# The end of a spectral-mix kernel: a tile's maximum and both of its products in one PSUM bank

## Chip, cores and metric

The kernel runs on one core of a Trainium2 chip. The metric is device time in microseconds (us): the median of several executions for the comparison, and one profiled execution for the trace. TensorE is called PE here, VectorE DVE, ScalarE ACT, GpSimd POOL; SP issues most transfers.

## What is computed

An attention over a sliding window with a linear position bias gives x; a spectral mix of 64 modes gives y; the end joins them. Cut to what matters (B 8, H 8, S 576, D 64, so 512 channels):

```python
x = attention(q, k, v)                    # window 128, bias by head; [8, 576, 512]
X = rfft(x, axis=1)[:, :64]               # 64 modes
Yr = Xr @ w_r - Xi @ w_i                  # one 512x512 matrix for each mode
Yi = Xr @ w_i + Xi @ w_r
y = irfft(Y, n=S, axis=1)
u = x + y
out = u + maximum(u @ w_ch, 0)            # fp32, [8, 576, 512]
```

The two weight tensors are 134 MB of fp32, read once; the output is 9.4 MB.

## The kernel before, in words

The first part is the attention by units of a head pair and a batch. Beside and after it the weights come through a ring of 12288 fp32 words a partition, each load two modes of one of w_r or w_i; `_load_w` issues a load on SP's queue as soon as `_modes` has used the place that it overwrites. `_modes` multiplies the chosen spectrum (Xz) by one load, 24 products into `acc`, and every few modes DVE adds `acc` into ZT, the spectrum of y laid out by channel.

During the weight stage the kernel does by the way what it can for the end. The output is 36 tiles of 128 rows by 512 channels (`g.seq`): for each batch four whole tiles, and for each two batches one tile of their two last half tiles. For each tile `_xt` transposes x and `_xw` multiplies it by w_ch; ACT and DVE split the result in two bf16 parts, high and low, and keep them in `hl`. `_z_early` turns the ZT of one batch into Z (rows are modes, columns channels) and ZW, which is Z times w_ch. The rows of the last modes are not there yet; they come as "late rows" after the last weights, for four batches at a time (`_z_late`), through a bf16 copy `zl` (`_z_late_out`), and `_z_put` copies 32 rows of it into place in Z and ZW.

With FT, the inverse transform, a tile's y is FT times Z and its y @ w_ch is FT times ZW. Products for a tile come in pairs, one for each half of 64 rows. A tile goes one of two ways (`g.way`):

- "a" (19 tiles): PE adds hl and FT times ZW in bank `mm`, and x (by the identity) and FT times Z in bank `y`: four pairs. ACT takes the relu of `mm`, DVE adds `y`.
- "q" (17 tiles): here x was added into hl already, by one identity product in `_xw`. PE makes `mm` from hl and FT times ZW, and `y` from FT times Z: three pairs. ACT copies `y`, DVE takes the maximum of `mm` and x (which is x + relu), POOL adds the two.

`_known` makes what needs no Z (lines 842 to 856), `_taken` what needs Z and ZW (829 to 839). The first two tiles (KNOWN) are made without the late rows in PE's idle time before the last weights, and the late rows added after. `_finish` (859 to 912) runs over the tiles in a hand-written order: every engine's queue is in the order of the code. The late rows of batches 0 to 3 are put by POOL, those of batches 4 to 7 are made after tile 7 (LATE_AT) and put by ACT and DVE at fixed tiles (PUT_Z). A "q" tile's transfer is issued after that of the next "a" tile.

Of the kernel before, what the change touches and what calls it, by code (L numbers as in the profile page):

```python
# [16 lines left out]
P = 128  # L17
# [9 lines left out]
TAIL = 2  # L27
XW = (20, 63)
EARLY_Z = (53, 55, 57, 58, 59, 60, 61, 62)
KNOWN = 2  # L30
FT_ROWS = (2, 3, 4, 5, 6)
FT_ORDERS = (10, 14, 18, 22)
WCH_ROWS = (1, 4)
PUT_Z = {4: 9, 5: 11, 6: 13, 7: 15}
LATE_AT = 7
SUMS = (P, 3 * P, 4 * P)


class Ctx:
# [4 lines left out]
def kernel(  # L44
# [44 lines left out]
    for b in range(B):  # L89
# [3 lines left out]
        if b == B - 1:  # L93
            t = [t[4], t[1], t[0], t[3], t[2]]
        g.seq += t
    g.way = ["q" if i > 4 and t[1][0][1] in SUMS and i != len(g.seq) - 5 else "a"
             for i, t in enumerate(g.seq)]

    with tc.manual_schedule(engines={ET.SP, ET.PE, ET.Activation, ET.DVE, ET.Pool}):
        with ExitStack() as wctx:  # L100
# [5 lines left out]
            with ExitStack() as actx:  # L106
# [87 lines left out]
                tc.tile_pool(name="eps", bufs=1, space=bass.MemoryType.PSUM))  # L194
            g.fps = ctx.enter_context(
                tc.tile_pool(name="fps", bufs=1, space=bass.MemoryType.PSUM))
            g.mm, g.y = {}, {}
            _select(g, last, 0)
            rest_w = [(m, w) for m in range(0, NM, 2) for w in range(2)]
            with ExitStack() as xctx:  # L200
# [28 lines left out]
            for m0, w in rest_w:  # L229
                _modes(g, last, m0, w, last=True)  # L230
                done = m0 + w + 1
                if done in EARLY_Z:
                    _z_early(g, EARLY_Z.index(done))
                if done == NM - 1:
                    for i in range(KNOWN):
                        _known(g, i)
                        _taken(g, i, last=False)
            _known(g, KNOWN, (1,))
            mctx.close()
        _finish(g)  # L240

# [319 lines left out]
def _select(g, j, m0):  # L561


    nc = g.nc
    A, H = len(GROUPS[j]), JOINT[j]
    pool = g.zp if j else g.work
    X = pool.tile([P, H * A, 3, MB, g.B], BF16, tag=f"Xz{j}", bufs=2, name=f"Xz{j}")
    per = H // len(GROUPS) if j else H
    for o0 in range(0, H, per):
        if j:  # L570
            ps = g.fps.tile([P, g.DM], FP32, tag=("mm", "y")[o0], name="xz")
        else:
            ps = g.ps2.tile([P, g.DM], FP32, tag="xt", name="xz")
        w = 2 * A * MB * g.B
        for o in range(per):
            q = ps[:, o * w : o * w + w].rearrange("p (c m b) -> p c m b", m=MB, b=g.B)
            for h in range(H):
                nc.tensor.matmul(  # L578
                    q[:, :, h::H], lhsT=g.sel[j][:, o0 + o, h],
                    rhs=g.Xn[j].rearrange("p c i b m -> p (c i) m b")[:, :, m0 + h : m0 + MB : H],  # L580
                    start=True, stop=True)
        q = ps[:, 0 : per * w].rearrange("p (c i m b) -> p c i m b", i=2, m=MB, b=g.B)
        r = slice(A * o0, A * (o0 + per))
        nc.vector.tensor_copy(X[:, r, 1:3], q)  # L584
        nc.scalar.mul(X[:, r, 0], q[:, :, 1], -1.0)  # L585
    g.X[j, m0 // MB] = X
# [58 lines left out]
def _load_w(g):  # L645
# [6 lines left out]
    for u, z in g.place[g.used : g.loaded]:  # L652
# [2 lines left out]
    g.loaded += 1  # L655
    r0 = GROUPS[j][0] * P
    src = (g.w_r, g.w_i)[w][m0 : m0 + JOINT[j], r0 : r0 + len(GROUPS[j]) * P]
    g.nc.sync.dma_start(
        out=g.ring[:, lo:hi], in_=src.rearrange("m (p a) e -> p m (a e)", a=ROWS[j]))
    return True  # L660


# [20 lines left out]
def _modes(g, j, m0, w, last=False):  # L683
# [9 lines left out]
        g.acc[j] = (m0, g.mpsum.tile([P, 4, 2, MB, 8], FP32, tag="acc", name="acc"))  # L693
    c0, acc = g.acc[j]
    R, n = ROWS[j], JOINT[j]
    for et in range(4):
        for a in range(R):
            nc.tensor.matmul(  # L698
                acc[:, et, :, m0 - c0 : m0 - c0 + n, :],
                lhsT=wt[:, a, et * P : (et + 1) * P],  # L700
                rhs=X[:, a, 1 - w : 3 - w, m0 % MB : m0 % MB + n],
                start=(m0 == c0 and w == et == a == 0),
                stop=(m0 + n in ends and w == 1 and et == 3 and a == R - 1))
    g.used += 1
    while _load_w(g):
        pass
# [36 lines left out]
def _xw(g, n, xT, psum):  # L743
# [2 lines left out]
    nc = g.nc  # L746
    x = g.seq[n][0]
    xw = psum.tile([P, g.DM], FP32, tag="xw", bufs=2, name="xw")
    if g.way[n] == "q":
        nc.tensor.matmul(xw, lhsT=g.ident_b, rhs=x, start=True, stop=False)  # L750
    for dt in range(4):
        nc.tensor.matmul(  # L752
            xw, lhsT=xT[:, dt], rhs=g.wch[:, dt],
            start=(dt == 0 and g.way[n] != "q"), stop=(dt == 3))
    for h in range(2):
        own, other = (slice(64 * i, 64 * i + 64) for i in (h, 1 - h))
        nc.scalar.copy(g.hl[own, n, h], xw[own])  # L757
# [4 lines left out]
def _z_early(g, b):  # L762
# [10 lines left out]
                _z_product(g, ps, w, et, k, l)  # L773
    nc.vector.tensor_copy(g.Z[b], zp.rearrange("p a b -> p (a b)"))
    nc.scalar.copy(g.ZW[b], zwp)  # L775
    if b == 0:
        nc.vector.memset(g.Z[b][0:32], 0.0)
        nc.gpsimd.memset(g.ZW[b][0:32], 0.0)  # L778


def _z_product(g, ps, w, et, k, l):
# [25 lines left out]
def _z_late_out(g, pool):  # L807

    nc = g.nc
    t = [pool.tile([P, g.DM], BF16, tag=f"zl{w}", bufs=1, name=f"zl{w}") for w in range(2)]  # L810
    nc.vector.tensor_copy(t[0], g.late[0])
    nc.scalar.copy(t[1], g.late[1])
    g.late = t


def _z_put(g, b):

    nc = g.nc
    ks = slice(32 * (b % 4), 32 * (b % 4) + 32)
    for z, t, odd in ((g.ZW, g.late[1], False), (g.Z, g.late[0], b % 2)):  # L820
        if b < 4:
            nc.gpsimd.tensor_copy(z[b][ks], t[ks])
        elif odd:
            nc.vector.tensor_copy(z[b][ks], t[ks])
        else:
            nc.scalar.copy(z[b][ks], t[ks])


def _taken(g, i, late=None, last=True):

    nc = g.nc
    rows = slice(0, 32) if late else slice(0, P)
    for w, out in ((1, g.mm[i]), (0, g.y[i])):
        for h, (b, s) in enumerate(g.seq[i][1]):
            z = late[w] if late else (g.Z, g.ZW)[w][b]
            nc.tensor.matmul(  # L836
                out[64 * h : 64 * h + 64], lhsT=g.FT[rows, b % 4, s : s + 64], rhs=z[rows],
                start=(w == 0 and g.way[i] == "q" and not late), stop=last,
                tile_position=(0, 64 * h))


def _known(g, i, which=(1, 0)):

    nc = g.nc
    x = g.seq[i][0]
    if 1 in which:
        pool = g.lps if i % 3 else g.fps
        g.mm[i] = pool.tile([P, g.DM], FP32, tag="mm", bufs=2 if i % 3 else 1, name="mm")
        _pair(nc, g.mm[i], [g.ident2] * 2, [g.hl[:, i, h] for h in range(2)],
              start=True, stop=False)  # L850
    if 0 in which:
        pool = g.fps if i % 3 == 0 else g.lps if i % 3 == 1 else g.kps
        g.y[i] = pool.tile([P, g.DM], FP32, tag="y", name="y")
        if g.way[i] == "a":
            _pair(nc, g.y[i], [g.ident_b[:, 0:64], g.ident_b[:, 64:128]], [x] * 2,
                  start=True, stop=False)


def _finish(g):

    nc, tc = g.nc, g.tc
    N = len(g.seq)
    with ExitStack() as fctx:
        pool = fctx.enter_context(tc.tile_pool(name="fin", bufs=4))
        g.kps = fctx.enter_context(
            tc.tile_pool(name="kps", bufs=1, space=bass.MemoryType.PSUM, side="right"))
        _z_late(g, 0)
        _known(g, KNOWN, (0,))  # L870
        _z_late_out(g, pool)
        first, ready = g.late, []
        for b in range(4):
            _z_put(g, b)
        for i in range(N + 1):
            if i < N:
                if i < KNOWN:
                    _taken(g, i, first)
                else:
                    if i > KNOWN:  # L880
                        _known(g, i)
                    _taken(g, i)
            if i == LATE_AT:
                _z_late(g, 4)
            j = i - 1
            if j < 0:
                continue
            x, (lo, hi) = g.seq[j]
            whole = hi == (lo[0], lo[1] + 64)
            oj = pool.tile([P, g.DM], FP32, tag="o", bufs=11, name="o")  # L890
            if g.way[j] == "a":
                r = pool.tile([P, g.DM], FP32, tag="r", name="r")
                nc.scalar.activation(r, g.mm[j], AF.Relu)
                nc.vector.tensor_tensor(out=oj, in0=g.y[j], in1=r, op=ALU.add)
            else:
                ys = pool.tile([P, g.DM], FP32, tag="y", name="ys")
                nc.scalar.copy(ys, g.y[j])
                r = pool.tile([P, g.DM], FP32, tag="r", name="r")
                nc.vector.tensor_tensor(out=r, in0=g.mm[j], in1=x, op=ALU.max)
                nc.gpsimd.tensor_tensor(out=oj, in0=r, in1=ys, op=ALU.add)  # L900
            ready.append((oj, lo, hi, whole))
            if g.way[j] == "a":
                for oj, lo, hi, whole in ready[-1:] + ready[:-1]:
                    if whole:
                        nc.sync.dma_start(out=g.out[lo[0], lo[1] : lo[1] + P], in_=oj)
                        continue
                    for h, (b, s) in enumerate((lo, hi)):
                        nc.sync.dma_start(out=g.out[b, s : s + 64], in_=oj[64 * h : 64 * h + 64])
                ready = []
            for b, at in PUT_Z.items():  # L910
                if j == at:
                    _z_put(g, b)


# [28 lines left out]
```

## Time and profile before

| what | us |
|---|---|
| median of 3 runs (452.98 to 454.67) | 454.45 |
| profiled execution, its time | 453.96 |
| its span | 452.2 |
| PE busy | 292.4 |
| DVE busy | 218.7 |
| ACT busy | 191.1 |
| POOL busy | 156.2 |
| HBM read, written | 163.58 MB, 9.44 MB |

The span is what the profiler saw from the first instruction to the last; the time of the execution holds 1.8 us more. A row of a group names the line, engine, operation and tiles, the shapes, the count, the busy time in us, the mean ns of one, and the idle time of the engine just before with what ended it. A row of a timeline begins with its start and its length in us from the span's start. A row of windows gives for each engine busy time and instructions in that stretch, and at its end the granted PE clock, the share of the 16 DMA engines that was busy, and GB/s. The chain of waits is followed back from the last instruction to what released each step.

### The profile page before, as it was taken

The numbers are of one execution on the slowest core, as the hardware profiler recorded it, in microseconds if no ns is written. First come the engines' busy times: TensorE is split into PE (matmuls) and PEld (weight loads), VectorE is DVE, ScalarE is ACT, GpSimd is POOL, SyncE is SP. The second block draws the span as 40 slices with busy tenths as digits, with TensorE's granted clock in tenths as the row PEclk, the third lists the DMA queues.
The fourth block names the chain that finished last, engine by engine and source line by source line (L and its number), as shares of the span: only waits on it lengthen the run. The fifth ranks groups of instructions, "written<-read, shape, count | busy, mean of one in ns | idle before, by whom it ended". The sixth has DMA issues, their size and how long they took to land.

```text
span 452.2 us, 12944 instructions
## 1 busy us (share of the span) xinstructions
PE 292.4 (65%) x5516; PEld 203.6 (45%) x5540; DVE 218.7 (48%) x434; ACT 191.1 (42%) x302; POOL 156.2 (35%) x265
## 2 busy tenths in 40 slices
PE   2668778986889883222322564757556667688994
PEld 2456566775767762211211343434333334455562
DVE  8457656676675561010000263635453536564784
ACT  4888567576675821000000141323232324343773
POOL 7799889787784502020000000000000000002785
PEclk9969868596795965555555588758896779999998
DMA  8999999999999999999999999999999999992778
GB/s 258 357 360 322 375 318 348 388 387 395 388 351 387 418 415 433 423 430 429 430 428 430 429 426 428 432 427 429 426 431 427 428 429 429 429 426 85 256 277 298
DMA packets 51273, 173.85 MB, mean 384 GB/s; under 512 B 4880, under 2 KB 21264, under 8 KB 43024
## 3 DMA queue, kind: packets, MB, share of 16 engines
q1 hardware_dynamic: 50832, 171.99, 96.0%
q0 software_dynamic: 384, 1.05, 0.9%
q8 instruction: 43, 0.70, 0.6%
q14 instruction: 14, 0.11, 0.1%
HBM read 163.58 MB, written 9.44 MB: 383 GB/s over the span
## 4 chain that ended last, share of the span: by engine, by line
DMA 60%; PE 21%; ACT 7%; DVE 5%; issue 3%; SPq 2%; POOL 2%; POOLq 0%; ACTq 0%; DVEq 0%
DMA ring<-in_moe_w_i_dram 33%; DMA ring<-in_moe_w_r_dram 19%; PE acc L698 4%; ACT att L459 4%; PE xt L539 3%; PE sc L447 3%; DMA v<-in_v_dram 3%; DMA q<-in_q_dram 3%; PE av L493 2%; DMA k<-in_k_dram 2%; ACT qkT L428 2%; PE tqk L420 2%; PE mm L836 1%; PE y L836 1%; PE mm L739 1%
## 5 line engine op out<-in xcount | busy, mean ns | idle before, releaser
L698 PE MATMUL acc<-Xz,ring 128*128 128x32 bf16 x2048 | 69.9, 183 | 107.4 <-DMA ring<-in_moe_w_i_dram 56.5
L698 PEld LDWEIGHTS <-ring 128*128 128x128 bf16 x2048 | 60.9, 101 | 137.7 <-DMA ring<-in_moe_w_i_dram 67.9
L757 ACT CAST hl<-xw 64x512 bf16<-64x512 f32 x72 | 41.8, 580 | 93.5 <-PE xw L752 61.6
L459 ACT ACTIVATE att<-sc 128x1024 bf16<-128x1024 f32 x64 | 65.6, 1025 | 29.7 <-PE sc L447 24.4
L758 DVE TENSOR_TENSOR hl<-xw,hl 64x512 bf16<-64x512 f32 x72 | 49.6, 688 | 55.3 <-ACT hl L757 54.8
L409 POOL CAST vb<-v 64x256 bf16<-64x256 f32 x128 | 64.1, 501 | 20.0 <-PE av L493 13.6
L778 POOL MEMSET ZTa<- 32x512 bf16 x1 | 0.5, 514 | 181.0 <-ACT ZTa L775 181.0
L447 PE MATMUL sc<-qkT,qkT 64*64 64x256 bf16 (+1 forms) x512 | 32.5, 333 | 26.4 <-ACT qkT L428 15.9
L752 PE MATMUL xw<-wch,xT 128*128 128x512 bf16 x133 | 44.5, 463 | 2.4 <-issue 1.5
L428 ACT COPY qkT<-tqk 128x576 bf16<-128x576 bf16 x64 | 40.6, 637 | 1.3 <-PE tqk L420 1.3
L420 PE MATMUL tqk<-ident_b,qkb 64*64 64x64 bf16 x1152 | 31.5, 214 | 9.3 <-POOL qkb L397 9.1
L420 PEld LDWEIGHTS <-qkb 64*64 64x64 bf16 x1152 | 30.8, 131 | 11.8 <-POOL qkb L397 11.1
L585 ACT ACTIVATE Xz<-xz 128x192 bf16<-128x192 f32 (+1 forms) x24 | 7.5, 313 | 63.8 <-DVE Xz L584 63.5
L464 DVE TENSOR_TENSOR att<-att,mask 128x1024 bf16<-128x1024 bf16 x32 | 27.2, 851 | 14.0 <-ACT att L459 13.5
L493 PE MATMUL av<-vb,att 128*128 128x65 bf16 (+1 forms) x512 | 31.4, 217 | 1.0 <-DVE att L469 0.8
L732 DVE COPY xT<-tp 128x512 bf16<-128x512 bf16 x36 | 15.1, 419 | 30.4 <-PE tp L730 30.0
L584 DVE CAST Xz<-xz 128x384 bf16<-128x384 f32 (+1 forms) x24 | 12.0, 512 | 34.2 <-PE xz L578 28.7
L397 POOL CAST qkb<-k 128x576 bf16<-128x576 f32 x32 | 28.4, 888 | 0.0
L493 PEld LDWEIGHTS <-att 128*128 128x128 bf16 (+1 forms) x512 | 24.8, 113 | 7.2 <-DVE att L469 1.3
L447 PEld LDWEIGHTS <-qkT 64*64 64x64 bf16 x512 | 13.4, 121 | 31.7 <-ACT qkT L428 18.4
L397 POOL CAST qkb<-q 128x576 bf16<-128x576 f32 x32 | 25.1, 785 | 6.2 <-PE tqk L420 3.1
L469 DVE TENSOR_TENSOR att<-att,mask 128x1024 bf16<-128x1024 bf16 x32 | 24.3, 759 | 1.5 <-ACT att L459 1.1
(110 smaller groups left out, 417.1 us busy)
## 6 DMA issues: line engine op xcount, KB each, us to landing
ring<-in_moe_w_r_dram SPq DMA_DIRECT2D x32, 1536.0 KB, 13.8
ring<-in_moe_w_i_dram SPq DMA_DIRECT2D x32, 1536.0 KB, 13.8
ring<-in_moe_w_r_dram SPq DMA_DIRECT2D x32, 512.0 KB, 7.0
ring<-in_moe_w_i_dram SPq DMA_DIRECT2D x32, 512.0 KB, 7.6
q<-in_q_dram SPq DMA_DIRECT2D x32, 288.0 KB, 6.5
k<-in_k_dram SPq DMA_DIRECT2D x32, 288.0 KB, 6.2
v<-in_v_dram SPq DMA_DIRECT2D x64, 128.0 KB, 5.9
out_dram<-o SPq DMA_DIRECT2D x32, 256.0 KB, 3.0
```

The costliest lines, as they stand in the source:

```text
L397: g.nc.gpsimd.tensor_copy(tb, t)
L409: g.nc.gpsimd.tensor_copy(o[64 * r : 64 * r + 64, i], v[64 * i : 64 * i + 64, r])
L420: g.nc.tensor.transpose(tp[hs, r, :], u.b[w][hs, r], g.ident_b[hs, hs], tile_position=(64 * hh, 64 * hh))
L428: g.nc.scalar.copy(dst.rearrange("c (p r) -> c p r", r=g.R), u.tp[w].rearrange("c r p -> c p r"))
L447: nc.tensor.matmul(sc[64 * r : 64 * r + 64, hh, 256 * i : 256 * i + nq], lhsT=kT[hs, c * P + r : c * P + P : 2], rhs=qT[hs, c * P : c * P ...
L459: nc.scalar.activation(a, sc, AF.Exp, scale=1.0 / math.sqrt(g.D))
L464: nc.vector.tensor_tensor(out=a, in0=a, in1=m, op=ALU.mult)
L493: nc.tensor.matmul(av[o, hh, col(t)], lhsT=att[c // 2][:, hh, q0 : q0 + m], rhs=u.vb[:, 2 * c + hh, 0 : D + 1], start=(j == 0), stop=(t < ...
L698: nc.tensor.matmul(acc[:, et, :, m0 - c0 : m0 - c0 + n, :], lhsT=wt[:, a, et * P : (et + 1) * P], rhs=X[:, a, 1 - w : 3 - w, m0 % MB : m0 ...
L752: nc.tensor.matmul(xw, lhsT=xT[:, dt], rhs=g.wch[:, dt], start=(dt == 0 and g.way[n] != "q"), stop=(dt == 3))
L757: nc.scalar.copy(g.hl[own, n, h], xw[own])
L758: nc.vector.tensor_tensor(out=g.hl[other, n, h], in0=xw[own], in1=g.hl[own, n, h], op=ALU.subtract)
```

## The change

All 36 tiles go one way. `_xw` adds x into hl by an identity product for every tile. A tile has one PSUM bank `u` of six: PE adds hl and FT times ZW there (x + x @ w_ch + y @ w_ch), DVE takes the maximum with x in place (x + relu), PE adds FT times Z onto it, ACT copies the result out to SBUF, SP issues its transfer, tile by tile in order. hl's and ZW's products stand four tiles ahead of Z's in PE's order; five tiles have theirs before the last weights. POOL puts all late rows; those of batches 4 to 7 are made after tile 6. The last weight load is issued as two halves, and the products behind it are ordered by half. Line numbers below the changed places move by some lines.

```diff
-KNOWN = 2
+KNOWN = 5
+AHEAD = 4
-LATE_AT = 7
+LATE_AT = 6
...
@@ _load_w
-    g.nc.sync.dma_start(
-        out=g.ring[:, lo:hi], in_=src.rearrange("m (p a) e -> p m (a e)", a=ROWS[j]))
+    a = ROWS[j]
+    n = 2 if g.loaded == len(g.parts) else 1
+    for i in range(n):
+        g.nc.sync.dma_start(
+            out=g.ring[:, lo + i * (hi - lo) // n : lo + (i + 1) * (hi - lo) // n],
+            in_=src.rearrange("m (p a) e -> p m (a e)", a=a)[
+                :, :, i * a * g.DM // n : (i + 1) * a * g.DM // n])
@@ _modes
+    order = [(et, a) for et in range(4) for a in range(R)]
+    if g.used == len(g.parts) - 1:
+        order = [(et, a) for h in (0, R // 2) for et in range(4) for a in range(h, h + R // 2)]
+    for et, a in order:
...
@@ _xw
-    if g.way[n] == "q":
-        nc.tensor.matmul(xw, lhsT=g.ident_b, rhs=x, start=True, stop=False)
+    nc.tensor.matmul(xw, lhsT=g.ident_b, rhs=x, start=True, stop=False)
...
@@ _z_early
-    if b == 0:
-        nc.vector.memset(g.Z[b][0:32], 0.0)
-        nc.gpsimd.memset(g.ZW[b][0:32], 0.0)
+    if b in {t[0] for i in range(KNOWN) for t in g.seq[i][1]}:
+        nc.gpsimd.memset(g.ZW[b][32 * (b % 4) : 32 * (b % 4) + 32], 0.0)
...
+def _z_put(g, w, b):
+    ks = slice(32 * (b % 4), 32 * (b % 4) + 32)
+    g.nc.gpsimd.tensor_copy((g.Z, g.ZW)[w][b][ks], g.late[w][ks])
+
+def _taken(g, i, w, late=None):
+    rows = slice(0, 32) if late else slice(0, P)
+    for h, (b, s) in enumerate(g.seq[i][1]):
+        o = slice(32 * (b % 4), 32 * (b % 4) + 32) if late else rows
+        z = late[w] if late else (g.Z, g.ZW)[w][b]
+        g.nc.tensor.matmul(
+            g.u[i][64 * h : 64 * h + 64], lhsT=g.FT[o, b % 4, s : s + 64], rhs=z[o],
+            start=False, stop=(w == 0 or late is not None or i >= KNOWN),
+            tile_position=(o.start, 64 * h), skip_group_check=(w == 0))
+
+def _known(g, i):
+    pool, tag = ((g.fps, "f0"), (g.fps, "f1"), (g.lps, "l0"), (g.lps, "l1"), (g.lps, "l2"),
+                 (g.kps, "k0"))[i % 6]
+    g.u[i] = pool.tile([P, g.DM], FP32, tag=tag, name="u")
+    _pair(g.nc, g.u[i], [g.ident2] * 2, [g.hl[:, i, h] for h in range(2)],
+          start=True, stop=False)
+
+def _greater(g, i):
+    g.nc.vector.tensor_tensor(out=g.u[i], in0=g.u[i], in1=g.seq[i][0], op=ALU.max)
@@ _finish
+        _z_late(g, 0)
+        _z_late_out(g, pool)
+        for w, b in ((0, 0), (1, 1), (0, 1), (1, 0), (1, 2), (0, 2), (1, 3), (0, 3)):
+            _z_put(g, w, b)
+        for i in range(KNOWN):
+            _taken(g, i, 1, g.late)
+            _greater(g, i)
+        for i in range(N):
+            _taken(g, i, 0)
+            n = i + AHEAD
+            if KNOWN <= n < N:
+                _known(g, n)
+                _taken(g, n, 1)
+                _greater(g, n)
+            if i == LATE_AT:
+                _z_late(g, 4)
+            o = pool.tile([P, g.DM], FP32, tag="o", name="o")
+            nc.scalar.copy(o, g.u[i])
+            _, (lo, hi) = g.seq[i]
+            if hi == (lo[0], lo[1] + 64):
+                nc.sync.dma_start(out=g.out[lo[0], lo[1] : lo[1] + P], in_=o)
+            else:
+                for h, (b, s) in enumerate((lo, hi)):
+                    nc.sync.dma_start(out=g.out[b, s : s + 64], in_=o[64 * h : 64 * h + 64])
+            if i == LATE_AT:
+                _z_late_out(g, pool)
+                for b in range(4, 8):
+                    for w in (1, 0):
+                        _z_put(g, w, b)
```

More of the change, by code (lines that the diff above doesn't have):

```diff
@@ L33 @@
 WCH_ROWS = (1, 4)
-PUT_Z = {4: 9, 5: 11, 6: 13, 7: 15}
-LATE_AT = 7
-SUMS = (P, 3 * P, 4 * P)
+LATE_AT = 6
 class Ctx:
@@ L95 @@
         g.seq += t
-    g.way = ["q" if i > 4 and t[1][0][1] in SUMS and i != len(g.seq) - 5 else "a"
-             for i, t in enumerate(g.seq)]
     with tc.manual_schedule(engines={ET.SP, ET.PE, ET.Activation, ET.DVE, ET.Pool}):
@@ L196 @@
                 tc.tile_pool(name="fps", bufs=1, space=bass.MemoryType.PSUM))
-            g.mm, g.y = {}, {}
+            g.u, g.kps = {}, None
             _select(g, last, 0)
@@ L236 @@
                         _known(g, i)
-                        _taken(g, i, last=False)
-            _known(g, KNOWN, (1,))
+                        _taken(g, i, 1)
             mctx.close()
@@ L570, in _select @@
         if j:
-            ps = g.fps.tile([P, g.DM], FP32, tag=("mm", "y")[o0], name="xz")
+            ps = g.fps.tile([P, g.DM], FP32, tag=f"f{o0}", name="xz")
         else:
@@ L695, in _modes @@
     R, n = ROWS[j], JOINT[j]
[L696 to L703, printed above, removed]
+    order = [(et, a) for et in range(4) for a in range(R)]
+    if g.used == len(g.parts) - 1:
+        order = [(et, a) for h in (0, R // 2) for et in range(4) for a in range(h, h + R // 2)]
+    for et, a in order:
+        nc.tensor.matmul(
+            acc[:, et, :, m0 - c0 : m0 - c0 + n, :],
+            lhsT=wt[:, a, et * P : (et + 1) * P],
+            rhs=X[:, a, 1 - w : 3 - w, m0 % MB : m0 % MB + n],
+            start=(m0 == c0 and w == 0 and (et, a) == order[0]),
+            stop=(m0 + n in ends and w == 1 and (et, a) == order[-1]))
     g.used += 1
@@ L748, in _xw @@
     xw = psum.tile([P, g.DM], FP32, tag="xw", bufs=2, name="xw")
-    if g.way[n] == "q":
-        nc.tensor.matmul(xw, lhsT=g.ident_b, rhs=x, start=True, stop=False)
+    nc.tensor.matmul(xw, lhsT=g.ident_b, rhs=x, start=True, stop=False)
     for dt in range(4):
         nc.tensor.matmul(
-            xw, lhsT=xT[:, dt], rhs=g.wch[:, dt],
-            start=(dt == 0 and g.way[n] != "q"), stop=(dt == 3))
+            xw, lhsT=xT[:, dt], rhs=g.wch[:, dt], start=False, stop=(dt == 3))
     for h in range(2):
@@ L809, in _z_late_out @@
     nc = g.nc
-    t = [pool.tile([P, g.DM], BF16, tag=f"zl{w}", bufs=1, name=f"zl{w}") for w in range(2)]
+    t = [pool.tile([P, g.DM], BF16, tag=f"zl{w}", bufs=2, name=f"zl{w}") for w in range(2)]
+    nc.scalar.copy(t[1], g.late[1])
     nc.vector.tensor_copy(t[0], g.late[0])
-    nc.scalar.copy(t[1], g.late[1])
     g.late = t
-def _z_put(g, b):
-    nc = g.nc
+def _z_put(g, w, b):
     ks = slice(32 * (b % 4), 32 * (b % 4) + 32)
[L820 to L826, printed above, removed]
@@ L829, in _taken @@
-def _taken(g, i, late=None, last=True):
-    nc = g.nc
-    rows = slice(0, 32) if late else slice(0, P)
[L833 to L839, printed above, removed]
@@ L842, in _known @@
[L842 to L856, printed above, removed]
+    g.nc.gpsimd.tensor_copy((g.Z, g.ZW)[w][b][ks], g.late[w][ks])
@@ L865, in _finish @@
     with ExitStack() as fctx:
-        pool = fctx.enter_context(tc.tile_pool(name="fin", bufs=4))
+        pool = fctx.enter_context(tc.tile_pool(name="fin", bufs=16))
         g.kps = fctx.enter_context(
@@ L869, in _finish @@
         _z_late(g, 0)
-        _known(g, KNOWN, (0,))
         _z_late_out(g, pool)
[L872 to L882, printed above, removed]
+        for w, b in ((0, 0), (1, 1), (0, 1), (1, 0), (1, 2), (0, 2), (1, 3), (0, 3)):
+            _z_put(g, w, b)
@@ L883, in _finish @@
+        for i in range(KNOWN):
[8 more added lines that the diff above has]
+                _greater(g, n)
             if i == LATE_AT:
                 _z_late(g, 4)
[L885 to L894, printed above, removed]
-            else:
[L896 to L912, printed above, removed]
+            o = pool.tile([P, g.DM], FP32, tag="o", name="o")
```

## The prediction, made before the changed kernel ran

> **What bounds the kernel now.** I read the page's slices first, then the chain of waits over the end, then the end grouped by operation and shape, then windows of the transfers.
>
> ```profile
> DMA  8999999999999999999999999999999999992778
> 398.63 13.77 DMA ring<-in_moe_w_i_dram
> 412.44 0.79 PE acc L698 x24
> 413.25 0.30 DVE ZT L723
> 413.60 1.12 PE zlw L785 x16
> 414.74 0.59 ACT zl L812
> 415.38 0.40 PE mm L836 x2
> ...
> 427.10 0.68 DVE ZTa L824
> 427.81 0.70 DVE r L899
> 428.56 0.41 PE mm L739 x2
> ...
> 442.13 3.55 DMA out_dram<-o
> ```
>
> The first line is the transfers' busy tenths in 40 slices of 11.3 us; the others (start, length, what) are the chain. Up to slice 36 the transfers are full: the kernel streams weights, and nothing in the change shortens that stream. The last weights are in use at 412.44. From there to the end of the span at 452.2 lie 39.8 us in which 36 tiles are finished and written; that is the stage to price. Its chain runs almost wholly through PE, and turns into a transfer only at 442.13.
>
> ```profile
> L900 POOL TENSOR_TENSOR o<-r,ys 128x512 f32<-128x512 f32 x17 | 21.4, 1271 | 5.4 <-DVE r L899 2.0 <-ACT r L893 2.0 <-ACT ys L897 1.1
> L739 PE MATMUL mm<-hl,ident 128*64 128x512 bf16 x68 | 13.7, 381 | 1.6 <-DVE r L899 1.6
> L897 ACT COPY ys<-y 128x512 f32<-128x512 f32 x17 | 9.9, 587 | 5.0 <-PE y L836 4.9
> L899 DVE TENSOR_TENSOR r<-mm,x_sb 128x512 f32<-128x512 f32 x14 | 9.6, 682 | 0.1
> L822 POOL COPY ZTa<-zl 32x512 bf16<-32x512 bf16 x8 | 4.6, 606 | 37.9 <-ACT zl L812 37.7
> 433.12 0.41 PE L739 MATMUL mm<-hl,ident 128*64 128x512 bf16 x2
> ...
> 433.99 0.41 PE L739 MATMUL mm<-hl,ident 128*64 128x512 bf16 x2
> 431.73 0.69 DVE L899 TENSOR_TENSOR r<-mm,x_sb 128x512 f32<-128x512 f32 x1
> 432.34 0.68 DVE L899 TENSOR_TENSOR r<-mm,x 128x512 f32<-128x512 f32 x1
> ```
>
> The groups give count, busy time, mean ns and idle time before; the other lines are the timeline. A pair of 64-row products starts every 0.216 us (433.12 to 433.99 in four steps, three rows left out between) and is complete 0.40 after its start. An "a" tile takes four pairs (0.86 us), a "q" tile three (0.65). DVE's rows last 0.69, but the next may start 0.61 after the one before it (431.73, 432.34): its rows overlap.
>
> ```profile
> 417.00:418.00 1.00, 1.00 (x12) 0.61 (x10) 1.00 (x3) 0.68 (x2) 0.94 (x3) 1.00 0.00 0
> 418.00:450.50 32.50, 25.85 (x256) 15.88 (x250) 23.03 (x36) 21.94 (x39) 23.59 (x21) 0.98 0.80 292
> 423.50:426.00 2.50, 2.50 (x28) 1.38 (x24) 1.40 (x3) 2.38 (x6) 1.40 (x3) 1.00 0.12 43
> 427.00:429.00 2.00, 1.06 (x11) 0.60 (x9) 1.94 (x4) 1.97 (x4) 0.56 (x2) 1.00 0.97 282
> 448.00:449.50 1.50, 0.00 (x0) 0.00 (x0) 0.00 (x0) 0.00 (x0) 0.00 (x0) 0.84 1.05 403
> 450.00:451.00 1.00, 0.00 (x0) 0.00 (x0) 0.00 (x0) 0.00 (x0) 0.00 (x0) 0.50 0.07 27
> 417.17 8.83 SPq L905 DMA_DIRECT2D out_dram<-o  x9
> 426.09 1.19 SPq L908 DMA_DIRECT2D out_dram<-o  x2
> ```
>
> The windows end with granted PE clock, DMA share and GB/s. Writing the output keeps the DMA engines busy for 0.80 of 32.5 us, 26.0 us; the other 6.5 they wait for tiles (0.12 busy at 423.5 to 426). At full share whole tiles move at 403 GB/s, 0.65 us for 262 KB. So 6.5 us at most is to be had while output transfers cost what they cost now.
>
> **The change part by part.** I call a tile's product of the identity with hl K, of FT with ZW W, of FT with Z Y. PE, then DVE's maximum in place, then PE's Y, then ACT's copy, all in one bank; six banks, K and W four tiles ahead of Y.
>
> *Last load in two halves.* The 24 products behind the last weights are 0.79; twelve now run beside the second half's landing, so 0.39 is saved. K and W of five tiles are ten pairs, 2.2 us, against eight before; they take part of PE's idle time ahead of the last weights:
>
> ```profile
> 411.07 0.38 PE L836 MATMUL y<-ZTa,FT 128*64 128x512 bf16 x2
> 412.44 0.78 PE L698 MATMUL acc<-Xz,ring 128*128 128x32 bf16 x24 [0.99 <-DMA ring<-in_moe_w_i_dram]
> 398.63 0.54 SPq L658 DMA_DIRECT2D ring<-in_moe_w_i_dram  x1
> 397.83 0.77 PE L698 MATMUL acc<-Xz,ring 128*128 128x32 bf16 x24 [0.28 <-DMA ring<-in_moe_w_i_dram]
> ```
>
> Two more pairs (0.43) fit under 0.99. The second half's issue costs SP another 0.54, but that is 14 us before it lands; bounds for the landing 0 to 0.54 late, I take 0.
>
> *x into hl by the identity for every tile.* Nineteen products more, each some 0.22, in the weight stage. A "q" phase with its identity product already ran with 0.28 us idle before the next weights (the 397.83 row); the others become like it. Cost 0, at most some tenths if that cover goes.
>
> *To the first tile.*
>
> ```profile
> 414.98 0.69 DVE L811 CAST zl<-zlp 128x512 bf16<-128x512 f32 x1 [1.44 <-PE zlp L789]
> 415.45 3.04 POOL L822 COPY ZTa<-zl 32x512 bf16<-32x512 bf16 x5 [37.69 <-ACT zl L812]
> ```
>
> The late rows' product starts at 413.21 (0.39 early). As in the chain, 1.78 later (413.60 to 415.38) the late W products start: 414.99. The pair ends at 415.39; maximum 0.69 with 0.04 hand-over: 416.12; Y, which also needs POOL's first put, ready by 416.0 (DVE's zl cast ended at 415.67 and now ends 0.39 earlier; hand-over 0.12, as from ACT's at 415.33 to 415.45; put 0.606): 416.18 to 416.58; ACT 0.59 with 0.04: 417.21; issue 417.25. Before, the first issue was at 417.17: nothing is gained there, 0.1 lost, because a tile now passes PE twice.
>
> *Rates from there.* PE: three pairs a tile, 0.65. DVE: one maximum a tile. Its output in PSUM is in no row of before: the nearest rows are L899 (PSUM and bf16 in, SBUF out) at 0.61 start to start; the other end is both passes through one bank in turn, 2 x 0.61 = 1.22. I take 0.61 to 0.69, since the operands are otherwise L899's. ACT: one copy, 0.59. POOL no longer adds (21.4 us gone); its 16 puts of 0.606 lie eight tiles ahead of their use for late batches, and the second is wanted at about 417 and done at 416.6. Transfers: 0.65 a tile, more for the four pairs of half tiles (0.97 share at 282 GB/s behind the halves at 426.09). So transfers, at 26.0 us for 36 tiles, 0.72, become the slowest of the five.
>
> The new waits: K of tile i+4 waits for ACT's copy of i-2, with W and the next Y behind it on PE. From that tile's Y to its copy's end is 0.40 + 0.04 + 0.59 + 0.06 = 1.09; six pairs lie between, 1.30. Hidden with 0.2 to spare. SP now waits for each tile in order; ACT's copy into an output buffer waits for a transfer 16 tiles back. Neither is late.
>
> *The late rows of batches 4 to 7* stay on PE, one tile earlier:
>
> ```profile
> 420.99 1.09 PE L785 MATMUL zlw<-wch,ZT 128*32 128x512 bf16 x16
> 421.90 0.42 PE L789 MATMUL zlp<-ident_b,ZT 128*32 128x128 bf16 x16
> 422.25 0.41 PE L739 MATMUL mm<-hl,ident 128*64 128x512 bf16 x2
> ```
>
> 1.26 us from the first start to the neighbour's, now ahead of tile 7's Y. Tile 7 comes 1.92 after tile 6, whose transfer takes 0.65: a hole of about 1.2 us in the transfers. The second casts of zl (ACT 0.59, DVE 0.69) fall in that hole. In the chain PE waits till 428.56 for L899, which stands behind DVE's cast of late rows at 427.10; such waits, 1.6 us in all, go, since POOL has those casts now. The like hole of before is the window at 423.5.
>
> *Sum.* First data 0.83 after the first issue (417.17, data from 418.0): 418.1. Plus 26.0 of transfers and 1.2 of hole: 445.3. Before, data ended at about 450.5, 1.7 before the span's end; so span 447.0, 5.2 less. PE alone: 103 pairs and 1.26 from 414.99 are done at 438.5; DVE at 0.69: 37 x 0.69 from 415.43 is 441.0, and 2.6 behind it (0.06 + 0.40 + 0.04 + 0.59 + 0.04 + 0.83 + 0.65) its last data, 443.6. Both are inside 445.3. The profiled execution took 453.96 with 1.8 outside the span: 448.8. The median of the runs, 454.45, is 0.5 above that execution; I say 449.0.
>
> A rule against this: the Trainium skill, Perfetto Trace Analysis, section Optimizing Scalar/DVE Operations, puts a DVE operation's data access at about 60 ns on SBUF and 125 on PSUM, about twice that in a profiled duration. By it the maximum, with its output moved to PSUM, would be 0.065 to 0.13 dearer than L899's rows, and DVE's last data would come at up to 445.4, level with the transfers: about 449.2. No run so far shows which holds.
>
> **Rivals.**
>
> *The bank loop or a dearer maximum sets the rate, still faster.* For: the slack on ACT's copy is 0.2 us a tile pair, and the maximum's price is unknown. At 0.80 us a tile DVE ends at 415.43 + 36 x 0.80 + 0.69 = 444.9, and 2.6 + 1.7 + 1.8 behind that is 451.0. Against: hand-overs of 0.04 to 0.06 in today's rows.
>
> *Slower: the maximum reads and writes the same bank and takes both passes in turn.* At 1.22 us it ends at 460.0, the time is 466.1. It decides from (447.9 - 415.43 - 0.69) / 36 = 0.88 us a maximum. For: no operation of before writes PSUM from DVE. Against: L899, with two operands, takes 682 ns, and the zl cast of the same shape, with one, 0.69: a second stream costs nothing there.
>
> *No change: output transfers are dearer when they follow one another.* At 282 to 300 GB/s all through, 9.44 MB take 31.5 to 33.5 us: data to about 450 to 452, time 453.5 to 455. For: the window at 427. Against: that window follows half tiles; the one at 448 is full at 403.
>
> **How the numbers follow.** As worked out: 0.60, its own range 447.2 to 450.4 (hole filled or not, landing, the maximum up to 0.75). Rate by the loop or DVE, 450.4 to 452: 0.13. Better than that, below 447.2: 0.04. No change: 0.09. The in-place maximum dear: 0.10; another loss, as a weight stage delayed by the identity products: 0.04. The range 446.5 to 453.0 holds eight in ten, leaving out the slow cases and part of the last. Half a per cent, 2.3 us, is about what a measurement of this kernel tells from no change: faster 0.77, same 0.09, slower 0.14.
>
> **What would show it.** Right: the first issue at 417.3 and not earlier; the maximum's rows at about 0.69 us, overlapping; three pairs a tile at 0.65 with no wait for ACT; DMA share near 1 from 424 on; one hole at about 423; data ending at about 445. Wrong: rows of the maximum of 0.9 us or more, PE waiting for it on every tile, or a full DMA share at under 350 GB/s; acc products after 412.44 that still run 24 in a row would take 0.4 back.

## The result, and the profile after

| | before | changed |
|---|---|---|
| median, us | 453.67 (8 runs) | 449.72 (8 runs, 447.59 to 451.92) |
| ratio of the two, 95% interval | | 0.9916 [0.9888, 0.9945] |
| the same again later | 453.53 (25 runs) | 449.00 (8 runs), ratio 0.9898 [0.9863, 0.9933] |
| profiled execution, its time | 453.96 | 449.20 |
| its span | 452.2 | 447.4 |

The forecast was 449.0 in 446.5 to 453.0, with 448.8 and a span of 447.0 for the profiled execution. Faster by 0.8 to 1.0%.

The chain of waits over the end of the changed kernel (start, length, what; steps of under 0.1 us left out):

```profile
412.16 0.48 PE acc L701 x12
412.66 0.30 DVE ZT L726
413.01 1.12 PE zlw L785 x16
414.15 0.60 ACT zl L811
414.79 1.06 PE u L828 x10
415.85 0.69 DVE u L845
416.57 0.41 PE u L828 x2
...
436.84 2.24 DMA out_dram<-o
439.08 0.97 ACT o L875 x2
```

Only 12 products stand behind the last weights. The chain still names PE for most of the end; the experiments show below that this must not be read as "PE sets the end". It stops at ACT's last copy (440.5), 5.3 us before the last data.

The end grouped by shape (count, busy us, mean ns, idle before), from the changed kernel:

```profile
L875 ACT COPY o<-u 128x512 f32<-128x512 f32 x36 | 20.8, 588 | 3.5 <-PE u L828 1.7
L845 DVE TENSOR_TENSOR u<-u,x_sb 128x512 f32<-128x512 f32 x32 | 20.6, 697 | 0.3
L742 PE MATMUL u<-hl,ident 128*64 128x512 bf16 x72 | 13.9, 380 | 0.0
L819 POOL COPY ZTa<-zl 32x512 bf16<-32x512 bf16 x12 | 7.1, 606 | 29.9 <-DVE zl L812 29.7
```

The maximum in place takes 697 ns, where the row nearest to it before, L899, took 682; K's products have no idle time ahead of them. From the timeline:

```profile
415.22 4.89 DVE L845 TENSOR_TENSOR u<-u,x_sb 128x512 f32<-128x512 f32 x8
422.09 0.38 PE L742 MATMUL u<-hl,ident 128*64 128x512 bf16 x2
422.74 0.38 PE L742 MATMUL u<-hl,ident 128*64 128x512 bf16 x2
423.38 0.38 PE L742 MATMUL u<-hl,ident 128*64 128x512 bf16 x2
417.04 6.20 SPq L878 DMA_DIRECT2D out_dram<-o  x8
441.45 2.04 SPq L878 DMA_DIRECT2D out_dram<-o  x4
```

Eight maxima in 4.89 us are (4.89 - 0.70) / 7 = 0.60 start to start. A tile takes PE 0.65. The first output is issued at 417.04. All of PE's waits from 409 on (us, times, longest) are these:

```profile
PE u L828 <- ACT zl L811: 0.4, 1, 0.4
PE u L828 <- DVE u L845: 0.4, 2, 0.2
PE zlw L785 <- DVE ZT L726: 0.4, 1, 0.4
PE acc L701 <- DMA ring<-in_moe_w_i_dram: 0.2, 1, 0.2
```

Windows of the changed kernel (busy us of PE, PE's loads, DVE, ACT and POOL with counts, then granted PE clock, DMA share, GB/s):

```profile
418.00:424.00 6.00, 6.00 (x78) 3.46 (x75) 5.79 (x10) 4.80 (x9) 3.58 (x7) 1.00 0.83 316
424.00:430.00 6.00, 6.00 (x58) 3.17 (x56) 6.00 (x11) 5.45 (x10) 3.08 (x6) 1.00 0.94 334
430.00:436.00 6.00, 6.00 (x60) 3.16 (x56) 6.00 (x10) 5.39 (x11) 0.00 (x0) 1.00 0.97 356
436.00:442.00 6.00, 3.28 (x30) 1.52 (x26) 3.04 (x5) 4.29 (x8) 0.00 (x0) 0.97 1.00 365
...
422.00:423.00 1.00, 1.00 (x12) 0.50 (x10) 0.87 (x2) 0.94 (x3) 0.63 (x2) 1.00 0.51 184
423.00:424.00 1.00, 1.00 (x12) 0.52 (x10) 1.00 (x2) 0.94 (x2) 0.94 (x2) 1.00 0.30 119
424.00:425.00 1.00, 1.00 (x12) 0.56 (x10) 1.00 (x3) 0.88 (x3) 0.94 (x3) 1.00 0.68 229
```

The same stretches of the kernel before:

```profile
424.00:430.00 6.00, 5.06 (x48) 2.95 (x46) 4.55 (x7) 5.90 (x12) 3.69 (x4) 1.00 0.65 217
430.00:436.00 6.00, 5.39 (x52) 3.25 (x47) 5.16 (x8) 4.66 (x9) 4.58 (x4) 1.00 0.69 266
436.00:442.00 6.00, 6.00 (x59) 4.13 (x57) 5.08 (x9) 4.64 (x9) 5.72 (x6) 1.00 0.89 306
```

Between 424 and 436 the share goes from two thirds to 0.94 and more. One hole is left, at 422 to 425, of 1.5 us: the late rows of batches 4 to 7.

Single executions of a kernel differ by 4 us and more; in the profiles the last weights land between 409.2 and 413.5. So the experiments are judged by a stage that leaves that out, from the end of the last weight packet to the end of the last output packet. These ends, and the service (all time of output packets divided by 16 engines), are added up from the trace's transfer records; "not served" is last data less first data less service.

```
kernel                     lands   first data  last data  service  not served  median us
                                   (both behind the landing)
before                     412.11     5.93      38.38     25.59      6.86       453.5
changed                    411.80     6.11      34.01     25.28      2.62       449.7
changed again  (e10)       411.62     6.14      33.76     25.21      2.41       449.0
half columns    (e1)       410.25     6.23      31.94     13.76       -         446.2
no hl           (e2)       413.51     6.14      33.07     25.16      1.77       448.1
ahead 2         (e3)       412.07     6.17      39.63     26.06      7.40       455.2
ahead 2, known 5 (e12)     411.81     6.14      37.14     26.06      4.95       453.0
one load        (e4)       411.57     6.52      35.03     25.38      3.13       450.0
before, no x    (e5)       412.78     6.70      40.84     26.00      8.14       454.5
before, no x late (e9)     410.79     5.95      38.21     26.05      6.21       452.1
late rows ACT/DVE (e6)     411.62     6.19      36.10     25.73      4.17       451.1
pair in one     (e7)       411.53     6.17      50.11     27.40       -         464.7
late rows at 11 (e8)       409.15     6.16      33.99     25.66      2.17       448.3
the same again (e11)       411.33     6.09      34.18     25.57      2.53       448.7
```

Of the stage's 4.4 us, 4.2 are time in which the transfers were not served (6.86 to 2.62), 0.3 is service, and the first data come 0.2 later. Two profiles of the changed kernel agree within 0.25 us; of the kernel before and of most others there is one. The medians were each taken beside runs of the kernel before, which had 453.0 to 453.7. The expectations up to e8, but for e4, count the stage from the first product on the last weights to the end of the span (39.8 us before, 35.2 changed), 1.2 to 1.4 more than the table; so only differences are compared there.

### The profile page after: what moved, and what is told of

It reads as the page before. It is cut to its first block, busy times and chain, and to the rows that moved or that the text cites. A ratio compares the mean times of both kernels' runs of the same rounds, so it can differ in the third digit from the quotient of the medians.

```text
span 447.4 us, 12904 instructions
## 1 busy us (share of the span) xinstructions
PE 291.3 (65%) x5523; PEld 200.3 (45%) x5523; DVE 219.6 (49%) x432; ACT 188.8 (42%) x297; POOL 138.5 (31%) x257
## 4 chain that ended last, share of the span: by engine, by line
DMA 51%; PE 22%; ACT 10%; DVE 8%; issue 4%; POOL 3%; ACTq 0%; SPq 0%; POOLq 0%
DMA ring<-in_moe_w_i_dram 31%; DMA ring<-in_moe_w_r_dram 19%; ACT att L455 6%; PE acc L701 4%; PE sc L443 4%; PE xt L535 3%; PE av L489 3%; ACT qkT L424 2%; PE u L828 2%; DMA out_dram<-o 1%; PE tqk L416 1%; POOL qkb L393 1%; DVE x_sb L503 1%; DVE att L465 1%; DVE att L460 1%
## 5 line engine op out<-in xcount | busy, mean ns | idle before, releaser
L405 POOL CAST vb<-v 64x256 bf16<-64x256 f32 x128 | 62.6, 489 | 21.3 <-PE av L489 13.7
L460 DVE TENSOR_TENSOR att<-att,mask 128x1024 bf16<-128x1024 bf16 x32 | 28.2, 880 | 13.0 <-ACT att L455 12.7
L393 POOL CAST qkb<-q 128x576 bf16<-128x576 f32 x32 | 27.0, 843 | 5.2 <-PE tqk L416 1.8
L393 POOL CAST qkb<-k 128x576 bf16<-128x576 f32 x32 | 25.9, 809 | 0.4 <-DMA k<-in_k_dram 0.3
L465 DVE TENSOR_TENSOR att<-att,mask 128x1024 bf16<-128x1024 bf16 x32 | 24.4, 763 | 1.5 <-ACT att L455 1.1
```

The costliest lines, as they stand in the source:

```text
L393: g.nc.gpsimd.tensor_copy(tb, t)
L405: g.nc.gpsimd.tensor_copy(o[64 * r : 64 * r + 64, i], v[64 * i : 64 * i + 64, r])
L460: nc.vector.tensor_tensor(out=a, in0=a, in1=m, op=ALU.mult)
```

## The experiments

**Half of each transfer.**

```diff
-nc.sync.dma_start(out=g.out[lo[0], lo[1] : lo[1] + P], in_=o)
+nc.sync.dma_start(out=g.out[lo[0], lo[1] : lo[1] + P, 0:256], in_=o[:, 0:256])
...      (the two halves of a pair tile likewise)
```

> The changed kernel, but each output transfer carries only 256 of the 512 columns, so half of the output is not written. Theory (after 424 us the output transfers are the last to end, and the other engines are done some 5 us before them): the last data no longer lag; they end about 1.5 us after ACT's last copy (440.5 in the changed kernel's profile), so the stage from the last weights' first product to the end of the span shrinks from 35.2 us to about 31, and the time falls by about 4 us. Rival (PE's order sets the end and the transfers follow it): ACT's last copy and the span stay, at most 0.7 us less.

The stage is 2.1 us shorter, between the two. (The median of four runs is 3.5 below the changed kernel's, nearer to the theory; in the profile the last weights also landed 1.5 earlier.) The end of its timeline:

```profile
435.75 3.35 ACT L875 COPY o<-u 128x512 f32<-128x512 f32 x6
437.95 1.11 SPq L881 DMA_DIRECT2D out_dram<-o  x2
439.15 2.03 SPq L878 DMA_DIRECT2D out_dram<-o  x4
```

ACT's last copy ends at 439.1, SP's last issue only at 441.2: the six issues from the last pair tile on take SP about half a microsecond each, and the last data end at 442.2. So in the changed kernel the transfers lag by 2.1 us over what SP's issues allow, and not by the 4 that I took. Issuing a part of the transfers from another engine was not tried.

**PE without hl's product.**

```diff
@@ _taken
-            start=False, stop=(w == 0 or late is not None or i >= KNOWN),
+            start=(w == 1 and i >= KNOWN), stop=(w == 0 or late is not None or i >= KNOWN),
@@ _known: takes the bank, and makes the product only with hl
-def _known(g, i):
+def _known(g, i, hl=True):
...
+    if hl:
...
@@ _finish
-                _known(g, n)
+                _known(g, n, False)
```

> The changed kernel without hl's product (x and x @ w_ch) for tiles 5 to 35 in the end: PE makes two pairs a tile there and not three, so the output of these tiles lacks that part. Theory (transfers last): PE has 31 x 0.216 = 6.7 us less to do, DVE becomes the pace at 0.61 a tile, but the transfers need 25.3 us of service whatever PE does; only the hole behind tile 6 may close a little. Stage 34.2 to 35.2 us, time 0 to 1 us less. Rival (PE sets the end): stage about 33 us or less, time 2 us or more lower.

0.9 us, with 6.7 us less for PE: as the theory had it. (The median is 1.6 below 449.7 and 0.9 below 449.0, of four runs that spread over 3.5 us.) Transfers and SP's issues, not PE, are last in the changed kernel.

**The distance between ZW's and Z's products.** First with both numbers changed (KNOWN 3, AHEAD 2):

> The changed kernel with hl's and ZW's products only two tiles ahead of Z's (KNOWN 3, AHEAD 2). Between a tile's ZW product and its Z product stand then four pairs, 0.86 us, while product, maximum and hand-overs take 0.40 + 0.04 + 0.69 + 0.06 = 1.19: PE waits for DVE and a tile takes about 0.81 us, not 0.65. Theory: PE and DVE end 5 to 6 us later, at about 445, and since the transfers lag by 5 us that costs only the part beyond their end: stage 36 to 37.5 us, time 1 to 2.5 us more. Rival (distance does not matter, PE keeps 0.65): no change. Other rival (PE sets the end): 5 to 6 us more.

It lost 5.6 us, as much as if PE set the end. Two things were mixed. The windows of that run show the first, in the clock:

```profile
414.67:418.08 3.41, 1.93 (x14) 0.75 (x16) 2.59 (x4) 1.56 (x3) 2.43 (x5) 1.00 0.00 0
418.00:420.00 2.00, 1.99 (x10) 1.18 (x11) 0.76 (x2) 0.58 (x1) 1.93 (x4) 0.52 0.68 262
420.00:422.00 2.00, 2.00 (x14) 1.14 (x11) 1.34 (x2) 0.94 (x2) 0.41 (x1) 0.63 0.43 169
```

PE, with K and W of three tiles and not five made early, was 57% busy in the 3.41 us up to 418.08, and then had half its clock for 3.4 us. So a run with AHEAD 2 alone:

```diff
-AHEAD = 4
+AHEAD = 2
```

> The changed kernel with AHEAD 2 again but KNOWN 5 kept, so that PE is as busy ahead of the last weights as in the changed kernel and its clock should stay at 1.00 (with KNOWN 3 it fell to 0.5 for 3.4 us). Theory: a tile behind the fifth takes 0.83 to 0.87 us, as in the run with KNOWN 3, because PE waits for DVE's maximum; now that the pace is slower than the transfers' 0.70 no lag builds up to hide it: stage from landing to last data 35.5 to 37 us, time 1.5 to 3 us above the changed kernel's. Rival (the loss of the run with KNOWN 3 was the clock's): within 0.7 us of the changed kernel.

3.1 us longer than the changed kernel (3.4 against its second profile), the clock at 1.00 as long as PE has work. PE's waits in this run (us, times, longest):

```profile
PE u L828 <- DVE u L845: 3.7, 16, 0.6
```

The theory of waiting for the maximum holds, a little above its range (37.1 where 37 was its upper end; the median 4.0 above that of e10, where 3 was the upper end). What fell is the idea behind the first expectation, that a lag of 5 us in the transfers would hide a slower PE: a lag builds up only while tiles come faster than they are written. At a slower pace there is none, and every tile's delay is paid.

**The last load in one piece.** `n = 1`, and the old order of products.

> The changed kernel with the last weight load in one piece and its 24 products in the old order. Theory: the late rows' product starts 0.3 to 0.4 us later behind the landing; span from the landing to the first output issue 0.3 to 0.4 us longer and all behind it the same; time up by 0.3 to 0.4 us, less than the timing tells. Rival (the second half's transfer costs what it saves): no shift of the landing and of the stage.

The first data come 6.52 behind the landing and not 6.11 to 6.14: 0.4, as predicted. That the stage is 1.0 longer is 0.6 more than that, and is not explained. The medians do not tell these apart.

**PE's fourth pair taken out of the kernel before.**

```diff
-                start=(w == 0 and g.way[i] == "q" and not late), stop=last,
+                start=(w == 0 and not late), stop=last,
...
-        if g.way[i] == "a":
-            _pair(nc, g.y[i], [g.ident_b[:, 0:64], g.ident_b[:, 64:128]], [x] * 2,
-                  start=True, stop=False)
```

> The kernel before without x's pair in bank y of the a tiles (their output lacks x): PE makes three pairs for every tile, as in the changed kernel, and nothing else changes. Theory A (the gain is PE's pair: 19 x 0.216 = 4.1 us): stage falls from 39.8 to 36 or 37 us, most of the change's gain. Theory B (the old ways through ACT, DVE and POOL, each a chain over two banks with casts of late rows between, hold PE up as soon as it is faster): stage falls by under 2 us, and PE shows more waits for DVE and ACT.

The stage got longer, in a profile that was the longest of ten executions (457.1; median 454.5). Again the clock:

```profile
414.00:416.00 2.00, 1.95 (x30) 1.04 (x32) 0.23 (x1) 0.05 (x1) 0.00 (x0) 0.67 0.05 12
416.00:418.00 2.00, 1.75 (x23) 0.73 (x12) 0.80 (x2) 1.14 (x2) 1.28 (x3) 0.50 0.00 0
418.00:420.00 2.00, 2.00 (x12) 0.72 (x10) 1.42 (x3) 1.20 (x2) 1.94 (x4) 0.50 0.26 103
```

So it was done again with the pairs ahead of the last weights kept:

```diff
-                start=(w == 0 and g.way[i] == "q" and not late), stop=last,
+                start=(w == 0 and i > KNOWN), stop=last,
...
-        if g.way[i] == "a":
+        if g.way[i] == "a" and i <= KNOWN:
```

> The kernel before without x's pair in bank y of the a tiles from the fourth on (their output lacks x); the three tiles in front of the late rows keep it, so PE is as busy ahead of the last weights as before. In the run without any of these pairs PE was granted half its clock from 414.7 to 421.5 us, which hid what the pairs cost. Theory A (the gain is PE's shorter work, 16 x 0.216 = 3.5 us): from the landing of the last weights to the last data 35 to 36 us, where the kernel before has 38.4 and the changed one 34.0. Theory B (two banks, three engines a tile and casts between them hold PE up as soon as it is faster): 37 to 38.4 us.

38.2 against 38.4: theory B. Windows of it, a row of its timeline and PE's waits in the end:

```profile
418.00:424.00 6.00, 6.00 (x76) 3.25 (x74) 4.13 (x7) 4.35 (x9) 5.10 (x6) 1.00 0.62 237
424.00:430.00 6.00, 4.14 (x34) 2.21 (x31) 5.14 (x8) 5.85 (x12) 3.48 (x3) 1.00 0.91 318
430.00:436.00 6.00, 5.75 (x52) 3.56 (x53) 5.61 (x10) 4.20 (x9) 5.67 (x5) 1.00 0.70 239
436.00:442.00 6.00, 5.89 (x53) 3.36 (x48) 5.48 (x10) 5.08 (x10) 6.00 (x6) 1.00 0.90 328
442.00:446.00 4.00, 0.01 (x1) 0.00 (x0) 1.17 (x2) 0.50 (x1) 1.91 (x2) 0.93 0.93 300
430.33 13.58 POOL L900 TENSOR_TENSOR o<-r,ys 128x512 f32<-128x512 f32 x11 [1.41 <-ACT r L893]
PE mm L739 <- DVE r L899: 2.1, 2, 1.0
```

PE is done at 442.0, 31.2 behind the landing; before, PE ran to 445.4, 33.3 behind. Those 2.1 us reach the last data as 0.2. The transfers were not served for 6.2 us in all: their share is 0.62 at 418 to 424 and 0.70 at 430 to 436, and in between PE is down to 4.14 of 6 us and waits for DVE. POOL adds without a gap for the last 13.6 us (before, 6.3 and 5.0 with 0.24 between). Which of these holds the stage up is read from the profile and not tested. The median, 452.1, is 1.4 below that of before beside it (453.5; ratio 0.9968 [0.9937, 0.9999]), so some gain there may be; the 3.5 us of theory A are in neither. PE's shorter work alone does not give the gain.

**Late rows of batches 4 to 7 by ACT and DVE**, as before, in the changed kernel:

```diff
+PUT_Z = {4: 9, 5: 11, 6: 13, 7: 15}
...
-            if i == LATE_AT:
-                _z_late_out(g, pool)
-                for b in range(4, 8):
-                    for w in (1, 0):
-                        _z_put(g, w, b)
+            for b, at in PUT_Z.items():
+                if i == at:
+                    ks = slice(32 * (b % 4), 32 * (b % 4) + 32)
+                    nc.scalar.copy(g.ZW[b][ks], g.late[1][ks])
+                    if b % 2:
+                        nc.vector.tensor_copy(g.Z[b][ks], g.late[0][ks])
+                    else:
+                        nc.scalar.copy(g.Z[b][ks], g.late[0][ks])
```

> The changed kernel with the late rows of batches 4 to 7 put by ACT (six casts) and DVE (two) from PSUM behind tiles 9, 11, 13 and 15, as before the change, in place of one cast each and POOL's eight puts. Theory: ACT, at 0.59 of 0.65 us a tile, has 2.3 us more to do between tiles 9 and 16, its copies come late, PE waits for the banks, and the transfers have a second hole: stage 1 to 2.5 us longer. Rival (the transfers lag enough to hide it): under 0.5 us.

2.1 us longer, as expected. ACT has no room:

```profile
424.00:430.00 6.00, 4.94 (x44) 2.67 (x42) 5.91 (x10) 5.88 (x13) 0.00 (x0) 1.00 0.82 284
PE u L743 <- ACT o L876: 1.3, 4, 0.7
```

PE is down to 4.94 of 6 us and waits for ACT's copies, the first time that the wait for a bank shows.

**The pair tiles in one transfer each.**

```diff
-                for h, (b, s) in enumerate((lo, hi)):
-                    nc.sync.dma_start(out=g.out[b, s : s + 64], in_=o[64 * h : 64 * h + 64])
+                nc.sync.dma_start(out=g.out[lo[0] : hi[0] + 1, lo[1] : lo[1] + 64], in_=o)
```

> The changed kernel with the four tiles of two half tiles written by one transfer of 128 rows each in place of two of 64. Theory: the halves cost the DMA engines 0.67 to 1.1 us a tile where whole tiles cost 0.67, since one transfer of 64 rows does not keep all the engines busy; in one transfer they cost 0.67 and SP saves four issues: the data end 0.7 to 1 us earlier, stage about 34.3 us. Rival (the cost is that of the addresses, or of what else is in the queue): no change.

Neither: 16 us longer. Two of its windows:

```profile
430.00:440.00 10.00, 9.07 (x84) 4.57 (x78) 8.83 (x14) 8.07 (x14) 0.00 (x0) 1.00 0.77 252
456.50:461.50 5.00, 0.00 (x0) 0.00 (x0) 0.00 (x0) 0.00 (x0) 0.00 (x0) 0.50 0.13 51
```

In the last 5 us 0.13 of the 16 engines, two of them on average, were still writing while the others had nothing left. Two is also the number of places in memory that such a transfer writes to; no run changes that number, so what spreads it so unevenly stays open. Why halves in two transfers cost more was not tested by this.

**The second late rows behind tile 11 and not 6** (`LATE_AT = 11`), twice:

> The changed kernel with the late rows of batches 4 to 7 made after tile 11 in place of tile 6. Theory: PE's 1.26 us for them leave a hole in the transfers only as far as the transfers have caught up; by tile 11 they lag by the pair tile's 0.4 us and some, so the hole shrinks by 0.4 to 0.8 us and the stage with it; ZW of batch 4 is wanted at tile 14, still in time. Rival (the rows come too late for tile 18's ZW product, PE waits for POOL): stage 0 to 2 us longer.

> The changed kernel once more, beside the next run on the same chip: from the landing of the last weights to the last data 34.0 us to within 0.5, data service 25.3 to 25.7, first data 6.1 behind the landing; time 449 to 450 us. If the stage differs by 1 us or more, differences of that size between the other runs tell nothing.

> The changed kernel with the late rows of batches 4 to 7 behind tile 11 once more, beside the run above. Theory: the hole is smaller and the stage 0.3 to 0.6 us shorter than the changed kernel's. Rival (the hole is only moved): the same within 0.2 us, as the first profile had it. Time 0 to 0.6 us below the changed kernel's.

33.99 and 34.18 against 34.01 and 33.76: no gain, as the second run's rival had it, the hole being only moved. The time not served is 2.2 to 2.5 in place of 2.4 to 2.6, and the service 0.3 to 0.4 more. The medians, 448.3 and 448.7 against 449.7 and 449.0, do not settle it either. No version tried beats the changed kernel clearly.

## Why the prediction was right, step by step

- *Last load in halves, 0.39.* DVE's ZT starts 0.86 behind the landing (412.66), before 1.14 (413.25): 0.28; in the run without the halves the first data come 0.4 later. Right in size, and by itself below what the medians tell.
- *Identity products in the weight stage, 0.* Nothing shows: the landing is at 411.80 and 411.62, before 412.11. But landings differ by 4 us between profiles, so some tenths would not show.
- *First issue at 417.25.* It came at 417.04, with the landing 0.3 earlier: 5.2 behind the landing, where 5.1 was forecast and before had 5.1. The first data lie 6.1 behind it, before 5.9.
- *The maximum at 0.61 to 0.69 start to start.* 0.60, and 697 ns in place of 682. Reading and writing one bank is not done in two passes; the slower rival is out. By the estimate from the Trainium skill, Perfetto Trace Analysis, section Optimizing Scalar/DVE Operations, read so that the output's place counts, 0.065 to 0.13 us more was to come; 0.015 came, and the measurement decides.
- *PE at 0.65 a tile without waiting for ACT; transfers last.* Right, but for SP, whose issues are last as soon as the transfers are lighter (e1): PE's waits in the end are 1.4 us in all, none for ACT's copies, and 6.7 us less work for PE bring 0.9.
- *A hole of 1.2 us.* 1.5 in the windows.
- *The sum, data end at 445.3.* It came at 445.8: 27.9 us of transfers with the hole where I had 27.2. Two terms were off and partly cancelled: 26.0 of service, taken from a rounded share of all transfers, where output packets alone have 25.3 (25.6 before), and 1.2 not served, where 2.6 came, since besides the hole 1.1 lie in small gaps. The forecast was 5.4 below the 454.45 then known; the medians came 4.0 and 4.5 below those of before. That 449.0 lies so near 449.72 and 449.00 is thus in part luck: the kernel before has 453.5 to 453.7 in more runs, and the gain was 0.7 to 0.8 of the forecast one. The rival of dearer transfers is out by the same 25.3.
- *What was misread.* "Its chain runs almost wholly through PE" reads as if PE's pairs set the end before. Alone they did not: with 3.5 us of them gone the last data came 0.2 earlier. The sum did not rest on this, since it was made from the transfers.
- *What was not priced.* That the order's distance carries most of it: with two tiles in place of four 3.1 of 4.4 us are lost, and with the late rows on ACT and DVE 2.1. These overlap and do not add up. What one bank a tile is worth apart from the distance that it makes room for was not tried, nor was the kernel before without POOL's adds or with its transfers issued tile by tile.

## What to carry to other kernels

When five engines and the transfers have nearly the same pace, the chain of waits names the one that happened to be last at each step. Price the stage by the resource that must do all of its work (here 25 us of output packets) and count in which stretches it is not fed. Shortening another engine then pays only if it feeds that resource earlier, and a lag hides a delay only while the producers are the faster ones.

## What was not expected of the hardware

- PE was granted half its clock for 6.83 us in e5 (from 414.69) and 3.41 in e3 (from 418.08), after 3.41 us in which it was 57% busy (a third time in e4, for 6.83 from 387.7 in the weight stage, after 54%). The Trainium skill, TensorE: Matmul & The Clock Gate, Part 1, has the windows of 3.4 us, which these lengths agree with; it asks for an idle window, and here a window little more than half busy was enough. But such a window does not always bring the fall: in e3 the 3.42 us before were 58% busy, in the kernel before PE was 53% busy from 384.2 to 391.0, and both times the clock stayed at 1.00. What decides is open. Of the fourteen profiles only e3 and e5, with fewer products ahead of or right behind the last weights, lose the clock while the tiles are made; so products that only fill a wait may pay by the clock, which is likely from this and not shown.
- Output transfers of 64 rows cost the engines 1.06 to 1.16 us a tile when little else was queued (e12), whole tiles 0.67; in a full queue (changed kernel) 0.8 to 1.1.
- One transfer to two places of 64 rows in memory cost 16 us over four tiles, as above.
